# Attention of the later blocks in nine stops of two chunks each, inside a y, instead of seventeen stops of one

## The chip, the cores and the metric

One core of a Trainium2 chip runs the whole program in one launch. The metric is the device time of one execution in microseconds (us), read as the median of several runs. One execution was also taken by the hardware profiler; all rows below are of that one.

## The reference, cut to what matters

A decaying linear attention feeds two dense layers with different activations. 1536 tokens, model width 512, inner width 2048.

```python
# attention: B=2, H=8, S=768, D=64, blocks of 64
intra = (q_b @ k_b.T * Dmask) @ v_b                 # Dmask[i,j] = lam**(i-j) for i >= j
inter = (q_b * lam**(i+1)) @ kv_state
out_b = intra + inter
kv_state = lam**64 * kv_state + (k_b * lam**(63-i)).T @ v_b
# layer 0
h = x @ w_in;  g = where(h > 0, h, exp(min(h, 0)) - 1);  x = g @ w_out
# layer 1
h = x @ w_in2; P = a0 + a1*h + a2*h**2 + a3*h**3; Q = 1 + |b0|*|h| + |b1|*h**2
y = (P / (Q + 1e-6)) @ w_out2
```

## The kernel before

**Tiling of the layers.** The tokens are cut into three blocks of 512 (t = 0, 1, 2), the inner width into 16 groups of 128 (f = 0 to 15). A step is one (layer, t, f). In it TensorE (PE) makes h, 128 inner features by 512 tokens, from the block's x (`mlp_h`, 12 matmuls, line 435), and then the y of the step two before (`LAG = 2`; `mlp_y`, 12 matmuls into four banks, line 517). Twelve, because every fp32 operand is split into a high and a low part and three of the four products are made. Between the two, ScalarE (ACT) and VectorE (DVE) turn h into g: lines 448 and 449 (relu and exp, ACT), 450 (b, DVE, the last reader of h's PSUM bank), 452 (high part, ACT) and 453 (low part, DVE). h alternates between two PSUM banks, y has four, and two more (`pa0`, `pa1`) serve the attention.

**Weights of layer 0.** They arrive as raw 64-bit words, a pair of halves per f (`load_pair`, 1 MB, line 122; it lands in one of two alternating slots). DVE makes fp32 of them in three passes (lines 78, 81, 84), ACT rounds the high part (line 127), DVE subtracts for the low part (line 128). All of this is done during t = 0, a step or two ahead of its use, together with parking half of layer 1's weights in DRAM during t = 1 (`park_w2`).

**Attention.** Block 0's attention is the start-up. That of blocks 1 and 2, 16 chunks of 64 tokens (8 to 23), runs during the steps of t = 0 and t = 1, in *stops* (`att_visit`): for a new chunk n the products k·q (line 340), for the chunk d of the stop before the products with v (line 345), k·v for the state (line 351) and state·q (line 356), each 8 matmuls of 64 x 64 on a 64 x 64 quarter of the array. Then DVE masks n's products (line 376), POOL multiplies n's q by its powers (line 371), ACT takes d's output out of PSUM (line 384) and DVE adds the state (line 388). Stops stand at the steps in

```python
visits = [(3, 5, 7, 9, 10, 12, 13, 14, 15), (2, 4, 6, 8, 10, 12, 14, 15)]
```

between a step's h and its y: 17 of them, the first with n alone, the last with d alone.

**Order.** The instructions of t = 0 and 1 stand in the order of the code (`manual_schedule`); each engine works its own queue in that order. SyncE (SP) issues all the transfers, also in order: one that waits for its buffer holds up all behind it. Attention's `kv` has two buffers, `qk` two (a `qk` holds two chunks).

Of the kernel before, what the change touches and what calls it, by code (L numbers as in the profile page):

```python
# [16 lines left out]
P = 128  # L17
# [12 lines left out]
def fused_kernel(ctx, tc, lam, qkv, w1, w2, ab, out):  # L30
# [16 lines left out]
    ph = ctx.enter_context(tc.tile_pool(name="ph", bufs=2, space=PSUM))  # L47
# [252 lines left out]
    aa_tiles = []  # L300

    def sm_load_qk(k):

        c, row = k // 2, 4 * P
        qk = qq.tile([P, NP, 2, C], F32, tag="qk", name=f"qk{c}")
        src = qkv[c, 0, 0]
        for rho, r in enumerate(ROWS):
            nc.sync.dma_start(
                out=qk[r].rearrange("p (g a) x i -> p g (a x i)", a=2),
                in_=bass.AP(src.tensor, src.offset + (1 - rho) * D * row,  # L310
                            [[row, D], [2 * P * row, NP // 2], [1, row]]))

        for b in range(2):
            chunk[k + b] = {"q": qk[:, :, 0, b * CS:(b + 1) * CS],
                            "k": qk[:, :, 1, (1 - b) * CS:(2 - b) * CS]}

    def sm_load_kv(k):
        c, b, row = k // 2, k % 2, 4 * P
        chunk[k]["kv"] = kv = qq.tile([P, NP, 2, D], F32, tag="kv", name=f"kv{k}")
# [7 lines left out]
    def sm_products(n, d):  # L327

        if not aa_tiles:
            aa_tiles.extend(pa.tile([P, T], F32, tag=f"pa{i}", name=f"aa{i}")  # L330
                            .rearrange("p (x m i) -> p x m i", x=2, m=NP) for i in range(2))
            for r in ROWS:
                nc.tensor.matmul(aa_tiles[1][r, 1], lhsT=pick[r], rhs=mask64[r, :, 1:CS + 1],  # L333
                                 start=True, stop=True, skip_group_check=True)
            nc.scalar.activation(out=qpow[:, :, 0:CS], in_=aa_tiles[1][:, 1], func=AF.Copy)
        pn, pd = chunk.get(n), chunk.get(d)
        for m in range(NP):
            if pn:
                for r in ROWS:
                    nc.tensor.matmul(aa_tiles[0][r, 0, m], lhsT=pn["k"][r, m],  # L340
                                     rhs=pn["q"][r, m], start=True, stop=True,
                                     skip_group_check=True)
            if pd:
                for i, r in enumerate(ROWS):
                    nc.tensor.matmul(aa_tiles[1][ROWS[1 - i], 0, m], lhsT=pd["kv"][r, m, 1],  # L345
                                     rhs=pd["s"][r, m], start=m == 0, stop=d % KB == 0,
                                     skip_group_check=True)
        for m in range(NP):
            if pd and d % KB < KB - 1:
                for r in ROWS:  # L350
                    nc.tensor.matmul(aa_tiles[0][r, 1, m], lhsT=pd["kv"][r, m, 0],  # L351
                                     rhs=pd["kv"][r, m, 1], start=True, stop=True,
                                     skip_group_check=True)
            if pd and d % KB:
                for i, r in enumerate(ROWS):
                    nc.tensor.matmul(aa_tiles[1][ROWS[1 - i], 0, m], lhsT=state[r, m, 0],  # L356
                                     rhs=pd["q"][r, m], start=False, stop=True,
                                     skip_group_check=True)

    def sm_decay_k(n):  # L360

        kv = chunk[n]["kv"]
        if n % KB < KB - 1:
# [4 lines left out]
    def sm_decay_q(n):  # L368
        q = chunk[n]["q"]
        if n % KB:  # L370
            nc.gpsimd.tensor_tensor(out=q, in0=q, in1=qpow[:, :, 0:CS], op=ALU.mult)

    def sm_mask(n):
        b = chunk[n]
        b["s"] = s = ap_.tile([P, NP, CS], F32, tag="s", name=f"s{n}")
        nc.vector.tensor_tensor(out=s, in0=aa_tiles[0][:, 0], in1=mask64[:, :, 0:CS], op=ALU.mult)

    def sm_out(d):

        t, js = d * CS // T, slice(d * CS % T, d * CS % T + CS)  # L380
        if t not in xraw:
            xraw[t] = xr.tile([P, NP, T], F32, tag="xr", name=f"xr{t}")
        first, last = d % KB == 0, d % KB == KB - 1
        nc.scalar.activation(out=xraw[t][:, :, js], in_=aa_tiles[1][:, 0], func=AF.Copy)
        if first:
            nc.scalar.activation(out=state[:, :, 0], in_=aa_tiles[0][:, 1], func=AF.Copy)
        elif not last:
            nc.vector.tensor_tensor(out=state[:, :, 0], in0=aa_tiles[0][:, 1],
                                    in1=state[:, :, 1], op=ALU.add)

    def sm_decay_state(d):

        if d % KB not in (0, KB - 1):
            for m in range(NP):
                nc.scalar.activation(out=state[:, m, 1], in_=state[:, m, 0], func=AF.Copy,
                                     scale=qpow[:, m, CS - 1:CS])

# [102 lines left out]
    def mlp_y(layer, t, f):  # L500
# [27 lines left out]
    with ExitStack() as actx:  # L528
# [4 lines left out]
        qq = actx.enter_context(tc.tile_pool(name="qq", bufs=2))  # L533

# [20 lines left out]
        dmask = ac.tile([P, H, C + 1], F32, name="dmask")  # L555
        qpow = ac.tile([P, NP, C], F32, name="qpow")
        state = ac.tile([P, NP, 2, D], F32, name="state")

        mask64 = dmask.rearrange("p (m h) i -> p m h i", h=2)[:, :, 1, CS:]
# [8 lines left out]
        def make_qpow():  # L568
# [5 lines left out]
            def double(n):  # L574
# [4 lines left out]
        yy, hh = ((py, "y"),) * 2, ((ph, "h"),) * 2  # L579
        pp = (yy, hh, yy, yy, hh, yy, yy, ((ph, "h"), (pa, "pa0")))  # L580
# [4 lines left out]
        loads = [[(sm_load_qk, first), (sm_load_kv, first)], [(sm_load_kv, first + 1)],  # L585
                 [(sm_load_qk, first + 2)]]
        loads += [[(sm_load_kv, k + 1)] + [(sm_load_qk, k + 2)] * (k % 2 == 0 and k + 2 < end)
                  for k in range(first + 1, end - 1)]
        with tc.manual_schedule():
# [17 lines left out]
            for load, k in loads.pop(0):  # L607
                load(k)
# [43 lines left out]
            for h in range(5, H):  # L652
# [14 lines left out]
            low(2)  # L667
            s_part(4)
# [24 lines left out]
            att_hand(*atts[6])  # L693
            low(7)
# [3 lines left out]
            nc.gpsimd.tensor_copy(  # L698
                out=mask64[ROWS[1]],
                in_=dmask.rearrange("p (m h) i -> p m h i", h=2)[ROWS[1], :, 0, 0:CS + 1])  # L700
# [3 lines left out]
        h_pool = lambda: (ph, "h")  # L704
# [8 lines left out]
        def att_visit(due, more):  # L713

            n = todo.pop(0) if more and todo else None
            d = due.pop() if due else None
            sm_products(n, d)
            if n is not None:
                sm_mask(n)
                sm_decay_q(n)  # L720
                due.append(n)
            if d is not None:
                sm_out(d)
                del chunk[d]

        with tc.manual_schedule():
            due = []
            next_d = []
# [6 lines left out]
            visits = [(3, 5, 7, 9, 10, 12, 13, 14, 15), (2, 4, 6, 8, 10, 12, 14, 15)]  # L735
            assert sum(park_at.values()) == len(parks)
            for layer, t, f in steps(0, 0) + steps(0, 1):
                if f == 0 and t:
# [3 lines left out]
                    for n in due:  # L742
                        sm_decay_k(n)
                new = mlp_h(layer, t, f, later=True)
                queue.append((layer, t, f))
                if t or f != 1:
                    run(old, 2)
                    for d in next_d:
                        sm_decay_state(d)
                    next_d = []  # L750
# [27 lines left out]
                if f in visits[t]:  # L778
                    att_visit(due, t == 0 or f < NF - 1)
                    next_d = list(due)  # L780
                    for n in due:
                        if f < NF - 1:
                            sm_decay_k(n)
                for w in now if t or f else ():
                    run(w, len(w) - 1)
                if t == 0 and f + 2 < FULL:
                    load_pair(f + 2)
                elif t == 0 and f in (FULL, NF - 2, NF - 1):
                    load_raw(2 if f == FULL else 1)
                elif t == 0 and f in (FULL - 2, FULL - 1, FULL + 1):  # L790
                    load_pair(*{FULL - 2: (FULL + 1, NF - 3), FULL - 1: (FULL + 2, NF - 4),
                                FULL + 1: (FULL + 3, NF - 3)}[f])
                if loads and (f in visits[t][1 - t:] or t == 0 and f in (1, 2)):
                    for load, k in loads.pop(0):
                        load(k)
                if t == 0 and f == 3:
                    load_raw(2)
                lows = [op for w in now for op in w]
                if len(queue) > LAG:
                    mlp_y(*queue.pop(0))  # L800
# [10 lines left out]
    def h_pool():  # L811
        nh[0] += 1
        return ((ph, "h"), (ph, "h"), (pa, "pa0"), (pa, "pa1"))[nh[0] % 4]
# [89 lines left out]
```

## Time and profile before

| | us |
|---|---|
| median of 3 runs | 573.3 |
| lowest and highest | 572.07, 573.34 |
| the profiled execution, its own time | 572.56 |
| its span, first to last instruction | 570.8 |

PE is busy 99% of the span at a granted clock of 0.999 of full speed; DVE 81%, ACT 63%, POOL 5%. In the page's 40 slices DVE reads 9 or more from the second to the ninth (14 to 128 us, most of t = 0), and 5 to 7 in t = 1. The profile's own page says that a busy PE is not PE at its peak, so the rows below look at starts, and at the distance from one start to the next.

### The profile page before, as it was taken

The numbers are of one execution on the slowest core, as the hardware profiler recorded it, in microseconds if no ns is written. First come the engines' busy times: TensorE is split into PE (matmuls) and PEld (weight loads), VectorE is DVE, ScalarE is ACT, GpSimd is POOL, SyncE is SP. The second block draws the span as 40 slices with busy tenths as digits, with TensorE's granted clock in tenths as the row PEclk, the third lists the DMA queues.
The fourth block names the chain that finished last, engine by engine and source line by source line (L and its number), as shares of the span: only waits on it lengthen the run. The fifth ranks groups of instructions, "written<-read, shape, count | busy, mean of one in ns | idle before, by whom it ended". The sixth has DMA issues, their size and how long they took to land.

```text
span 570.8 us, 9255 instructions
## 1 busy us (share of the span) xinstructions
PE 564.6 (99%) x3550; PEld 464.9 (81%) x3550; DVE 464.7 (81%) x722; ACT 358.5 (63%) x690; POOL 29.8 (5%) x51
## 2 busy tenths in 40 slices
PE   8999999999999999999999999999999999999997
PEld 7877888888888888888888888888888888888885
DVE  6999999965676635877979999888898888898882
ACT  3746646875554545555568976667877666776672
POOL 7401001100100000000000000000000000000000
PEclk9999999999999999999999999999999999999999
DMA  8977677464687513434432500000400000200001
GB/s 291 318 225 243 237 227 214 107 206 128 204 240 229 165 49 136 167 135 177 150 108 78 182 3 1 1 2 0 145 3 2 0 1 0 75 0 1 1 1 74
DMA packets 41215, 64.58 MB, mean 113 GB/s; under 512 B 20178, under 2 KB 20178, under 8 KB 41170
## 3 DMA queue, kind: packets, MB, share of 16 engines
q1 hardware_dynamic: 41168, 63.98, 35.8%
q8 instruction: 28, 0.46, 0.3%
q14 instruction: 17, 0.14, 0.1%
q10 hardware_dynamic: 2, 0.00, 0.0%
HBM read 53.48 MB, written 10.49 MB: 112 GB/s over the span
## 4 chain that ended last, share of the span: by engine, by line
PE 98%; DMA 1%; SPq 0%; ACT 0%; issue 0%
PE h L435 46%; PE y L517 43%; PE y L426 3%; PE aa L340 1%; DMA att<-qkv_in 1%; PE aa L351 1%; PE pa L243 1%; PE pa L209 1%; PE pa L249 0%; PE aa L356 0%; PE aa L345 0%; SPq L192 0%; PE sums L256 0%; PE pa L291 0%; ACT o L487 0%; PE aa L333 0%
## 5 line engine op out<-in xcount | busy, mean ns | idle before, releaser
L435 PE MATMUL h<-xhi,w 128*128 128x512 f32 x768 | 204.8, 389 | 0.0
L517 PE MATMUL y<-ghi,w 128*128 128x512 f32 x712 | 191.8, 392 | 0.0
L435 PEld LDWEIGHTS h<-xhi,w 128*128 128x128 f32 x768 | 143.8, 188 | 30.3 <-DVE w L128 0.4
L517 PEld LDWEIGHTS y<-ghi,w 128*128 128x128 f32 x712 | 132.3, 188 | 27.8
L435 PE MATMUL h<-xlo,w 128*128 128x512 f32 x384 | 102.6, 389 | 0.0
L517 PE MATMUL y<-glo,w 128*128 128x512 f32 x356 | 95.3, 389 | 0.0
L435 PEld LDWEIGHTS h<-xlo,w 128*128 128x128 f32 x384 | 72.1, 188 | 15.0
L517 PEld LDWEIGHTS y<-glo,w 128*128 128x128 f32 x356 | 66.8, 188 | 14.2
L461 ACT ACTIVATE a<-h,babs 128x512 f32<-128x512 f32 x48 | 33.0, 688 | 63.8 <-PE h L435 63.8
L448 ACT ACTIVATE a<-h 128x512 f32<-128x512 f32 x48 | 28.3, 589 | 43.1 <-PE h L435 42.9
L465 DVE SCALAR_TENSOR_TENSOR b<-b,babs,a 128x512 f32<-128x512 f32 x48 | 36.0, 751 | 20.9 <-ACT b L462 20.7
L450 DVE SCALAR_TENSOR_TENSOR b<-a,h 128x512 f32<-128x512 f32 x48 | 32.7, 681 | 15.3 <-ACT a L449 12.1
L452 ACT ACTIVATE ghi<-b 128x512 fp32r<-128x512 f32 x48 | 30.0, 626 | 22.4 <-DVE b L450 22.4
L453 DVE TENSOR_TENSOR glo<-b,ghi 128x512 fp32r<-128x512 f32 x48 | 34.0, 709 | 7.0 <-ACT ghi L452 4.8
L463 ACT ACTIVATE p<-h,cab 128x512 f32<-128x512 f32 x48 | 37.7, 785 | 0.0
L467 ACT ACTIVATE a<-b,one 128x512 f32<-128x512 f32 x48 | 35.0, 729 | 3.1 <-DVE b L465 2.6
L469 DVE SCALAR_TENSOR_TENSOR p<-p,cab,h 128x512 f32<-128x512 f32 x48 | 35.8, 746 | 1.2
L473 DVE SCALAR_TENSOR_TENSOR b<-b,one,a 128x512 f32<-128x512 f32 x48 | 35.8, 746 | 0.1
L475 DVE SCALAR_TENSOR_TENSOR p<-p,cab,a 128x512 f32<-128x512 f32 x48 | 35.8, 746 | 0.0
L58 DVE TENSOR_TENSOR glo<-p,ghi 128x512 fp32r<-128x512 f32 x48 | 33.0, 688 | 3.0 <-PE y L426 1.5
L468 DVE TENSOR_TENSOR p<-p,h 128x512 f32<-128x512 f32 x48 | 32.8, 682 | 2.9 <-ACT p L463 2.9
L477 DVE SCALAR_TENSOR_TENSOR p<-b,p 128x512 f32<-128x512 f32 x48 | 33.1, 690 | 1.2
(88 smaller groups left out, 611.2 us busy)
## 6 DMA issues: line engine op xcount, KB each, us to landing
raw<-w_in SPq DMA_DIRECT2D x64, 512.0 KB, 4.5
att<-qkv_in SPq DMA_DIRECT2D x16, 256.0 KB, 6.0
qk<-qkv_in SPq DMA_DIRECT2D x16, 256.0 KB, 4.3
kv<-qkv_in SPq DMA_DIRECT2D x64, 64.0 KB, 4.0
w2d<-wbuf SPq DMA_DIRECT2D x16, 256.0 KB, 4.5
wbuf<-w2d SPq DMA_DIRECT2D x16, 256.0 KB, 2.8
x2d<-o SPq DMA_DIRECT2D x12, 256.0 KB, 2.3
x2r<-x2d SPq DMA_DIRECT2D x12, 256.0 KB, 3.1
```

Of the source, the lines that this page charges most:

```text
L58: lo_eng.tensor_tensor(out=lo, in0=src, in1=hi.bitcast(F32), op=ALU.subtract)
L435: nc.tensor.matmul(h, lhsT=w[:, a, 0, k * P:(k + 1) * P], rhs=xs[layer, t, k][b], start=i == k == 0, stop=i == 2 and k == NP - 1)
L453: lambda: nc.vector.tensor_tensor(out=glo, in0=b, in1=ghi.bitcast(F32), op=ALU.subtract)]
L461: nc.scalar.activation(out=a, in_=h, func=AF.Abs, scale=babs[:, 0:1])
L463: nc.scalar.activation(out=p, in_=h, func=AF.Identity, scale=cab[:, 3:4], bias=cab[:, 2:3])
L465: nc.vector.scalar_tensor_tensor(out=b, in0=b, scalar=babs[:, 1:2], in1=a, op0=ALU.mult, op1=ALU.add)
L467: nc.scalar.activation(out=a, in_=b, func=AF.Ln, bias=one[:, 0:1])
L469: nc.vector.scalar_tensor_tensor(out=p, in0=p, scalar=cab[:, 1:2], in1=h, op0=ALU.add, op1=ALU.mult)
L473: nc.vector.scalar_tensor_tensor(out=b, in0=b, scalar=one[:, 0:1], in1=a, op0=ALU.add, op1=ALU.mult)
L475: nc.vector.scalar_tensor_tensor(out=p, in0=p, scalar=cab[:, 0:1], in1=a, op0=ALU.add, op1=ALU.mult)
L477: nc.vector.scalar_tensor_tensor(out=p, in0=b, scalar=2.0, in1=p, op0=ALU.subtract, op1=ALU.mult, reverse0=True)
L517: nc.tensor.matmul(ys[layer, t][m], lhsT=w[:, a, 1, m * P:(m + 1) * P], rhs=g[b], start=f == i == 0, stop=False)
```

## The change

`att_visit` takes two chunks n, n+1 and the two of the stop before. Stops stand at nine steps, `at = [2, 5, 8, 11, 14, 18, 22, 26, 30]` counted over t = 0 and 1, and no more between h and y but inside `mlp_y`, after the seventh of its 12 matmuls. The outputs of the older pair go to the spare h bank (`ax`, the bank that the next step's h will take), so both banks of `pa` serve the new pair's k·q (`pa0`) and the k·v (`pa1`). Masks and q's decay are one instruction per pair, the output copy too; the state is added in two instructions, the second a step later (`sm_state`), and k·v of a chunk is made at the stop of the next pair. A table of powers (`pow64`) that the first stop made is made in the start-up (`sm_banks`). `kv` has three buffers.

At a stop's step the transfers of the next attention pair stand ahead of that step's raw weights (`load_w1`).

```diff
-    ph = ctx.enter_context(tc.tile_pool(name="ph", bufs=2, space=PSUM))
+    ph = ctx.enter_context(tc.tile_pool(name="ph", bufs=1, space=PSUM))
...
+    def sm_products(n, d, spare):
+
+        if d is not None:
+            aa_x[0] = spare.rearrange("p (m x i) -> p m x i", x=2, m=NP)
+        for j in range(2):
+            pn = chunk.get(n + j) if n is not None else None
+            pd = chunk.get(d + j) if d is not None else None
+            for m in range(NP):
+                if pn:
+                    for r in ROWS:
+                        nc.tensor.matmul(aa_tiles[1][r, j, m], lhsT=pn["k"][r, m],
+                                         rhs=pn["q"][r, m], start=True, stop=True,
+                                         skip_group_check=True)
+                if pd:
+                    for i, r in enumerate(ROWS):
+                        nc.tensor.matmul(aa_x[0][ROWS[1 - i], m, j], lhsT=pd["kv"][r, m, 1],
+                                         rhs=pd["s"][r, m], start=j == m == 0,
+                                         stop=(d + j) % KB == 0, skip_group_check=True)
+        for j in range(2):
+            c = n + j - 1 if n is not None else None
+            kv = chunk[c]["kv"] if c in chunk and c % KB < KB - 1 else None
...
     def sm_decay_q(n):
-        q = chunk[n]["q"]
-        if n % KB:
-            nc.gpsimd.tensor_tensor(out=q, in0=q, in1=qpow[:, :, 0:CS], op=ALU.mult)
+        q = chunk[n]["qk"][:, :, 0].rearrange("p m (b i) -> p m b i", b=2)
+        nc.gpsimd.tensor_tensor(
+            out=q, in0=q, in1=pow64.rearrange("p m (b i) -> p m b i", b=1)
+            .to_broadcast([P, NP, 2, CS]), op=ALU.mult)
...
+        nc.scalar.activation(out=xraw[t][:, :, js].rearrange("p m (b i) -> p m b i", b=2),
+                             in_=aa_x[0], func=AF.Copy)
...
-    def mlp_y(layer, t, f):
+    def mlp_y(layer, t, f, between=None):
...
+                if between and (i, m) == (1, 2):
+                    between()
...
+        vv = actx.enter_context(tc.tile_pool(name="vv", bufs=3))
...
+        at = [2, 5, 8, 11, 14, NF + 2, NF + 6, NF + 10, NF + 14]
+        pairs = list(range(first, end, 2))
+        loads = {}
+        for i, k in enumerate(pairs[1:]):
+            for j, load in enumerate(((sm_load_kv, k - 1), (sm_load_qk, k), (sm_load_kv, k))):
+                loads.setdefault(at[i] if i or j else 1, []).append(load)
...
+        def att_visit(s, f):
+
+            v = at.index(s)
+            spare = ph.tile([P, T], F32, tag=f"h{(f + 1) % 2}", name=f"ax{s}") if v else None
...
                 for w in now if t or f else ():
-                    run(w, len(w) - 1)
...
+                    run(w, len(w) - (2 if s in at else 1))
+                if s not in at:
+                    load_w1(t, f)
+                if len(queue) > LAG:
+                    mlp_y(*queue.pop(0), between=(lambda: att_visit(s, f)) if s in at else None)
...
+                for load, k in loads.get(s, ()):
+                    load(k)
+                if s in at:
+                    load_w1(t, f)
```

PE's queue around the first stop, before (a row is line, operation, out<-in, size; `aa` is a bank of `pa`):

```order
L435 MATMUL h_0_3_586<-xhi_0_0_261,w_1_508 128x512 x2
L435 MATMUL h_0_3_586<-xhi_0_1_285,w_1_508 128x512 x2
L333 MATMUL aa_613<-dmask,tabs 64x256 x2
L340 MATMUL aa_612<-qk_200 64x64 x8
L517 MATMUL y_0_0_570<-ghi_0_1_504,w_1_508 128x512
L517 MATMUL y_0_1_571<-ghi_0_1_504,w_1_508 128x512
```

And PE's queue around the first stop now, in step 2 (line 346 is k·q, 361 is k·v, 535 is y, 453 is h):

```order
L535 MATMUL y_0_2_579<-ghi_0_0_490,w_0_222 128x512
L535 MATMUL y_0_3_580<-ghi_0_0_490,w_0_222 128x512
L535 MATMUL y_0_0_577<-glo_0_0_491,w_0_222 128x512
L535 MATMUL y_0_1_578<-glo_0_0_491,w_0_222 128x512
L535 MATMUL y_0_2_579<-glo_0_0_491,w_0_222 128x512
L346 MATMUL aa_533<-qk_204 64x64 x16
L361 MATMUL aa_462<-kv_207 64x64 x8
L535 MATMUL y_0_3_580<-glo_0_0_491,w_0_222 128x512
L535 MATMUL y_0_0_577<-ghi_0_0_490,w_0_222 128x512
L535 MATMUL y_0_1_578<-ghi_0_0_490,w_0_222 128x512
```

The 8 small matmuls between h and y became 24 behind the seventh matmul of a y, and the two of line 333 stand in the start-up.

SP's queue from the first `kv` issued in the layers' steps to the raw weights of f = 8, before:

```order
L323 DMA kv_530<-qkv_in 64x4x64 x4
L122 DMA raw_4_564<-w_in 128x1024 x2
L308 DMA qk_567<-qkv_in 64x2x512 x2
L122 DMA raw_5_635<-w_in 128x1024 x2
L114 DMA raw_12_0_638<-w_in 128x1024
L114 DMA raw_10_1_640<-w_in 128x1024
L122 DMA raw_6_687<-w_in 128x1024 x2
L122 DMA raw_7_773<-w_in 128x1024 x2
L323 DMA kv_776<-qkv_in 64x4x64 x4
L122 DMA raw_8_826<-w_in 128x1024 x2
```

The same stretch of SP's queue now:

```order
L323 DMA kv_544<-qkv_in 64x4x64 x4
L308 DMA qk_621<-qkv_in 64x2x512 x2
L323 DMA kv_624<-qkv_in 64x4x64 x4
L122 DMA raw_4_629<-w_in 128x1024 x2
L122 DMA raw_5_666<-w_in 128x1024 x2
L122 DMA raw_6_722<-w_in 128x1024 x2
L323 DMA kv_849<-qkv_in 64x4x64 x4
L308 DMA qk_854<-qkv_in 64x2x512 x2
L323 DMA kv_857<-qkv_in 64x4x64 x4
L122 DMA raw_7_862<-w_in 128x1024 x2
L122 DMA raw_8_899<-w_in 128x1024 x2
```

raw_4 and raw_7 (the number is f) now stand behind six and ten issues of attention's inputs.

## Rows read from the trace of the kernel before

**Rows 1.** The page, part 4: the chain that ended last.
```profile
PE 98%; DMA 1%; SPq 0%; ACT 0%; issue 0%
```

**Rows 2.** Waits, PE's weight loads (engine, line, releaser: us in total, times, longest).
```profile
PEld aa L340 <- issue: 4.9, 14, 0.4
PEld h L435 <- DVE w L128: 0.4, 1, 0.4
```

**Rows 3.** Timeline, PE, the stop of step 7 (start us, duration us, engine, line).
```profile
59.12 1.07 PE L435 MATMUL h<-xhi,w 128*128 128x512 f32 x4
...
60.23 0.23 PE L340 MATMUL aa<-qk 64*64 64x64 f32 x2
...
61.05 0.23 PE L351 MATMUL aa<-kv 64*64 64x64 f32 x2
...
61.22 1.19 PE L517 MATMUL y<-ghi,w 128*128 128x512 f32 x4
62.25 1.08 PE L517 MATMUL y<-glo,w 128*128 128x512 f32 x4
```

**Rows 4.** The chain in order of time, two y of t = 0 (start us, us).
```profile
42.29 2.72 PE y L517 x12
...
61.28 2.95 PE y L517 x12
```

**Rows 5.** Instructions on tile aa, k·q (count of records; duration ns least, median, most).
```profile
L340 PE MATMUL aa<-qk x256: 215/218/267, 36.0 to 202.9; 64*64 64x64 f32 x128
```

**Rows 6.** Timeline, PE, the first stop.
```profile
35.51 0.65 PE L333 MATMUL aa<-dmask,tabs 64*64 64x256 f32 x4
35.99 0.63 PE L340 MATMUL aa<-qk 64*64 64x64 f32 x16
```

**Rows 7.** Timeline, PE and ACT, the last stop.
```profile
209.15 0.68 PE L345 MATMUL aa<-s,kv 64*64 64x64 f32 x16
209.26 0.60 ACT L448 ACTIVATE a<-h 128x512 f32<-128x512 f32 x1 [3.66 <-PE h L435]
...
210.42 0.37 ACT L384 ACTIVATE xr<-aa 128x256 f32<-128x256 f32 x1
```

**Rows 8.** Timeline, DVE, steps 4 to 7 (the bracket: idle before, and its releaser).
```profile
44.88 0.70 DVE L78 TENSOR_SCALAR w<-raw 128x1024 int32<-128x1024 int32 x1 [1.26 <-DMA raw<-w_in]
...
49.62 0.68 DVE L450 SCALAR_TENSOR_TENSOR b<-a,h 128x512 f32<-128x512 f32 x1
...
52.58 0.42 DVE L376 TENSOR_TENSOR s<-aa,dmask 128x256 f32<-128x256 f32 x1
52.92 0.42 DVE L388 TENSOR_TENSOR state<-aa,state 128x256 f32<-128x256 f32 x1
...
56.24 0.69 DVE L78 TENSOR_SCALAR w<-raw 128x1024 int32<-128x1024 int32 x1
...
61.59 0.68 DVE L78 TENSOR_SCALAR w<-raw 128x1024 int32<-128x1024 int32 x1
```

**Rows 9.** Timeline, SP's queue: issues of raw weights, qk and kv.
```profile
32.29 2.50 SPq L323 DMA_DIRECT2D kv<-qkv_in  x4
36.80 1.34 SPq L122 DMA_DIRECT2D raw<-w_in  x2
38.19 1.27 SPq L308 DMA_DIRECT2D qk<-qkv_in  x2
...
49.73 6.83 SPq L122 DMA_DIRECT2D raw<-w_in  x4
56.66 2.51 SPq L323 DMA_DIRECT2D kv<-qkv_in  x4
```

**Rows 10.** Transfers of line 122: from issue to landing.
```profile
DMA to landing us min/median/max: 3.1/4.8/10.0
```

**Rows 11.** Timeline, POOL and DVE beside each other in t = 1.
```profile
191.02 0.73 POOL L371 TENSOR_TENSOR qk<-qk,qpow 128x256 f32<-128x256 f32 x1 [11.28 <-PE aa L340]
...
191.05 1.25 DVE L453 TENSOR_TENSOR glo<-b,ghi 128x512 fp32r<-128x512 f32 x1
```

More of the change, by code (lines that the diff above doesn't have):

```diff
@@ L325, in sm_load_kv @@
                     [[row, CS], [P, 4], [1, D]]))
[L327 to L358, printed above, removed]
@@ L360, in sm_decay_k @@
     def sm_decay_k(n):
-        kv = chunk[n]["kv"]
-        if n % KB < KB - 1:
+        if n in chunk and n % KB < KB - 1:
+            kv = chunk[n]["kv"]
             for m in range(NP):
@@ L381, in sm_out @@
         if t not in xraw:
             xraw[t] = xr.tile([P, NP, T], F32, tag="xr", name=f"xr{t}")
[L383 to L389, printed above, removed]
@@ L391, in sm_decay_state, with sm_state @@
-    def sm_decay_state(d):
-        if d % KB not in (0, KB - 1):
+        nc.scalar.activation(out=xraw[t][:, :, js].rearrange("p m (b i) -> p m b i", b=2),
+                             in_=aa_x[0], func=AF.Copy)
+    def sm_state(n):
+        if n - 1 in chunk and n % KB:
+            j = n % 2
+            if n % KB == 1:
+                nc.scalar.activation(out=state[:, :, j], in_=aa_tiles[0][:, j], func=AF.Copy)
+            else:
+                nc.vector.tensor_tensor(out=state[:, :, j], in0=aa_tiles[0][:, j],
+                                        in1=state[:, :, 2], op=ALU.add)
@@ L584, in fused_kernel @@
         first, end = todo[0], todo[-1] + 1
[L585 to L588, printed above, removed]
+        at = [2, 5, 8, 11, 14, NF + 2, NF + 6, NF + 10, NF + 14]
[4 more added lines that the diff above has]
+                loads.setdefault(at[i] if i or j else 1, []).append(load)
+        loads.setdefault(at[-2], []).append((sm_load_kv, end - 1))
+        work, late, states = {}, {}, {}
+        for v, s in enumerate(at[:-1]):
+            k = first + 2 * v
+            if v:
+                late.setdefault(s - 1, []).extend((sm_decay_k, n) for n in (k - 1, k))
+            work.setdefault(s + 1, []).append((sm_decay_state, k))
+            states[s + 1] = k + 1
+            work.setdefault(s + 2 + (s + 2 == NF), []).append((sm_decay_state, k + 1))
         with tc.manual_schedule():
@@ L606, in fused_kernel @@
             load_pair(1)
-            for load, k in loads.pop(0):
-                load(k)
+            for load in (sm_load_qk, sm_load_kv):
+                load(first)
             def s_part(i):
@@ L693, in fused_kernel @@
             att_hand(*atts[6])
+            sm_banks()
             low(7)
@@ L711, in fused_kernel @@
         queue = []
[L713 to L717, printed above, removed]
+        def att_visit(s, f):
+            v = at.index(s)
+            spare = ph.tile([P, T], F32, tag=f"h{(f + 1) % 2}", name=f"ax{s}") if v else None
+            n = pairs[v] if v < len(pairs) else None
+            d = pairs[v - 1] if v else None
+            sm_products(n, d, spare)
+            if d is not None:
+                sm_out(d)
             if n is not None:
@@ L720, in att_visit @@
                 sm_decay_q(n)
-                due.append(n)
             if d is not None:
-                sm_out(d)
-                del chunk[d]
+                if n is not None:
+                    sm_state(n)
+                for j in range(2):
+                    del chunk[d + j]
         with tc.manual_schedule():
-            due = []
-            next_d = []
             lows = w
```

117 lines of the change are left out of this document (71 added, 46 removed).

## The prediction

> **What bounds the kernel now.** I read the chain that ended last first: PE holds 98% of it [rows 1], so only what shortens PE's queue, or makes PE wait, moves the time. Then the waits of PE: outside the start-up its weight loads wait for another engine once, for 0.4 us; the larger item is 4.9 us of "issue" in front of the first k·q matmul of 14 stops, 0.35 us each [rows 2]. So something is paid each time PE turns from the large matmuls to the small ones, though nothing is late. Third, the timeline of one stop, to price it. 12 large matmuls take 2.72 us [rows 4], 0.227 each. The last four of h start at 59.12, so without a stop y would begin at 60.03. Its fifth matmul starts at 62.25, where 60.03 + 4 x 0.227 = 60.94 was due: a full stop costs 1.31 us. Of that, the small matmuls go in pairs, one pair every 0.0586 us (14 spacings from 60.23 to 61.05), 16 pairs, 0.94 us; 0.37 us is left that does not depend on how many there are, before the first and around the return to y [rows 3]. Call a pair's place a slot. A matmul without a partner takes a slot too: the last stop's 8 matmuls with v (16 records) stand alone and are busy 0.68 us, less one duration of 0.22 that is 0.46 for 7.5 slots, 0.06 each [rows 5, 7].
>
> **The sum.** Before: 16 records per stop, 256 records, so 16 stops with k·q [rows 5], and one more with d alone; 17 in all. Slots: 16 x 16 + 8 = 264. With the table of powers in the first stop, 0.48 us from its start to that of k·q [rows 6]: 17 x 0.37 + 264 x 0.0586 + 0.48 = 6.29 + 15.47 + 0.48 = 22.24 us.
> After: nine stops. The first has 16 k·q and 8 k·v, none with a partner of the other kind: 24 slots. The other seven with new chunks have 16 + 16 paired and 16 more: 32. The last has 16 and 16 alone: 32. That is 280. 9 x 0.37 + 280 x 0.0586 = 3.33 + 16.41 = 19.74, and the table 0.48 in the start-up, where PE works on into the first h: 20.22 us.
> Difference: -2.02 us, which is 8 x 0.37 less 16 x 0.0586. Two places are not in the trace. The table in the start-up: nothing if PE would have waited there anyhow, at most another 0.37 if it makes a turn of its own; I take its 0.48. The turn inside a y instead of between h and y: the same change of matmuls on both sides, so 0.37; bounds 0.25 and 0.5, what one turn shows when the 0.12 lost on the return's four matmuls (1.03 for 0.91) is left out or paid twice, which is 1.1 us either way over nine stops.
>
> **What the small engines gain or lose, and what hides it.** Output copy: 16 ACT copies of 256 columns become 8 of 512. The masks on DVE: 16 of 0.34 (start to next start) become 8 of at most 0.68; the 13 state adds of 0.34 stay [rows 8]; POOL's 15 of 0.73 become 8 of about 1.46. A step with a weight pair costs DVE 5.35 us (from line 78 to the next, 56.24 to 61.59) against PE's 5.44. In three steps with one stop DVE has 16.05 + 0.68 + 0.68 = 17.4, PE 16.3 + 2.25 = 18.6, so DVE still gains 1.2 us on PE per stop. I cost all this at nothing. The cover is thin at three new meetings of queues.
>
> *The spare bank before the stop.* At stop s the products with v write the bank that h of step s-1 had, so they wait for b of step s-1 on DVE (line 450). Before, that b had until the next h, a stop and a y later. Behind PE's waiting matmul stands everything. Stop 5: in the old trace y ends and h5 begins at 45.01 [rows 4], and h5 ends at 47.73; by then the new kernel has paid 0.48 + 1.78 for the table and stop 2 instead of 0.48 + 0.84 for the first stop, so h5 ends at 48.67 and the bank is wanted 7 x 0.227 + 0.1 later, 50.4. b of step 4 ended at 49.62 + 0.68 = 50.30. DVE has 0.68 more in front of it (a pair's mask for a chunk's, and a state add), which goes into the 1.26 us in which it waited for the raw weights of f = 4, until 44.88 [rows 8]. So no stall, if those weights land as before. They are now issued behind qk and kv: 32.29 + 2.50 + 1.27 + 2.51 = 38.6 instead of 36.80 [rows 9], but qk, which followed and shared the engines with them, is then already away. Bounds of the landing: 0.7 us earlier (median of 4.8 behind the second issue at 39.4 [rows 10]) to 1.8 later; of the stall: 0 to 1.7. I take 0, near the median.
>
> *The raw weights behind the attention.* At stop 5 the kv and qk transfers need buffers that the stop's own products free, from about 51.0; they take 2.5 + 1.27 + 2.5 us of SP, so the pair of f = 7 goes out at 57.3 to 58.0, where it ended at 56.56 before, and lands 4.8 after the second issue at 57.65, at 62.4 [rows 9, 10]. DVE wants it at 61.59 plus the 0.68 that stop 5 adds, 62.3. b of step 7 then ends one step of 5.35 on, at 67.8. Stop 8 wants the bank at: h8 ends in the old trace at 61.28 + 2.95 + 2.72 = 66.95, shifted by 0.48 + 1.78 + 2.25 - 3.94 = +0.57, and 1.7 us on: 69.2. Slack 1.4 us. The pairs of stops 8 and 11 stand likewise. This slack is used up when a pair lands later than 6.2 us from issue; the measured longest is 10.0.
>
> *The spare bank after the stop.* The next h takes the bank as soon as the five last matmuls of y are through, 1.13 us plus about 0.1 after the products. ACT starts such a copy 0.1 us behind the products' end, and 512 columns from PSUM take 0.60 [rows 7]: 0.7 us. It is ready 0.5 us early, unless ACT is behind, and ACT is behind only when b was.
>
> POOL stands between. In the trace a DVE subtraction that started just behind POOL's 0.73 us product took 1.25 us [rows 11], where 512 columns take 0.68 [rows 8]: 0.57 lost to the overlap. With the doubled product the loss at one meeting lies between that 0.57 and 1.3 (1.46 less the same remainder); there are fewer meetings. I take the smaller, inside DVE's 1.2 us per stop.
> The Trainium skill, "SBUF — State Buffer", section "SBUF: two separate sides", says that the port pair of VectorE and GpSimd is an exclusive lock held for a whole instruction. The row agrees (DVE went on only after POOL's end), and by that rule the longer instruction costs DVE the 1.3, 0.7 more per meeting.
> At stop 5 the larger loss would leave 0.68 + 0.7 against 1.26 of cover, a stall of about 0.1.
>
> **Forecast.** -2.0 us on PE's queue, nothing else on the path: 572.56 - 2.0 = 570.5 in the profiled execution, which lies 0.7 under the median of 573.3; against that median 571.3. 0.3%, 1.7 us, is about what can be told from no change, so the forecast lies just beyond it. Its own range is 570.2 to 572.4, by the bounds of the turn.
>
> **Rivals.**
> 1. *DVE late at the spare bank*: the weights of f = 4 land by their later issue, or the lock takes more, and PE stalls about 1 us at stop 5, with remainders later. For it: no slack in the sum at stop 5. Against it: DVE's 1.2 us per stop. 573.3 - 2.0 + 1.0 = 572.3, within 0.3%.
> 2. *SP's queue makes PE wait; slower.* If the pairs behind the attention land midway between median and longest, 7.4 us from issue, each of stops 8, 11 and 14 meets a b that is 1.2 us late (7.4 less 6.2), 3.6 us together: 573.3 - 2.0 + 3.6 = 574.9. It decides from 6.2 us on; gain and loss cancel at 6.9. For it: f = 4 landed at 44.88, 7.4 us behind the second issue (36.80 + 0.67), when qk shared the engines. Against: now the attention goes first and is mostly moved before the pair starts.
> 3. *The change doesn't save the turns*: 0.37 belongs to 16 slots and not to a stop. Then 280 slots cost 0.94 more and nothing is saved: 574.2. Against it: the second half of a stop begins without a gap, one pair behind the other through 61.05 [rows 3], and the first stop with 8 slots paid a turn like the others.
>
> **Chances.** Forecast 0.50, rival 1 0.30, rival 2 0.14, rival 3 0.06. Faster by over 0.3%: 0.48, nearly all of the forecast. Within 0.3%: 0.36, rival 1 and what of the forecast and of rival 2 falls short. Slower by over 0.3%: 0.16, from rival 2, and rival 3 when it is at its worst. The range of 570.2 to 574.3 leaves out the upper half of rival 2 and little below.
>
> **What would show it.** Right: nine groups of small matmuls, about 2.25 us each from the seventh to the eighth matmul of a y beyond 0.23; "issue" in front of k·q falls from 14 x 0.35 to about 8; y and h groups of 2.72 everywhere else. Rival 1: PE's first matmul with v, or the h behind a stop, waits for DVE's b or ACT's output copy, at step 5 first. Rival 2: DVE's line 78 waits for raw weights at steps 7, 11 and 13 by over 1 us, and PE stands in the next stop. Rival 3: stops of 2.6 us and more with no releaser. The forecast is wrong if h0 itself begins over 0.8 us later, or if PE waits for over 0.5 us in all during t = 0 and 1.

## The result and the profile after

The changed kernel takes 575.5 us (median of 4 runs, 575.18 to 576.33), the kernel before 573.1 beside it (572.07 to 573.34): 1.0057 of its time, interval 1.0045 to 1.007. It is 2.4 us slower where 2.0 faster was forecast. The profiled execution has a span of 573.4 us, before 570.8, so 2.6 are to be found in it.

The chain that ended last, page part 4; before, PE held 98% of it [rows 1]:

```profile
PE 84%; DVE 8%; DMA 2%; SPq 2%; issue 1%; ACT 1%; DVEq 0%
```

A seventh of the chain has gone over to DVE and to what DVE waits for. Where, the waits of PE's weight loads tell (in total, times, longest); against them stand the two rows of before [rows 2]:

```profile
PEld aa L346 <- issue: 2.5, 7, 0.4
PEld ax L351 <- DVE b L468: 1.9, 3, 0.8
...
PEld y L535 <- ACT o L505: 1.1, 4, 0.3
PEld h L453 <- ACT xhi L57: 1.0, 3, 0.3
PEld h L453 <- DVE w L128: 0.5, 1, 0.5
```

The first row is the gain: 7 turns in front of k·q instead of 14 (the other two of the nine stops, and three of the seventeen before, are booked under other names, 0.35 to 0.4 us each). The other four are new or larger, 4.5 us; two small ones (0.4 for b in front of an h at 218 us, 0.2 for xlo) make it 5.1. Less the 0.4 that waited before and the 2.0 of the forecast, 2.7 is left, the 2.6 of the spans.

The gain itself is there. The timeline of PE, the stop of step 22, where nothing is late:

```profile
156.95 1.07 PE L535 MATMUL y<-ghi,w 128*128 128x512 f32 x4
157.85 0.84 PE L535 MATMUL y<-glo,w 128*128 128x512 f32 x3
158.63 0.27 PE L346 MATMUL aa<-qk 64*64 64x64 f32 x2
...
160.65 0.50 PE L535 MATMUL y<-glo,w 128*128 128x512 f32 x1
160.99 1.09 PE L535 MATMUL y<-ghi,w 128*128 128x512 f32 x4
```

The ninth matmul of this y was due at 156.95 + 8 x 0.227 = 158.77 and begins at 160.99: a stop of 2.22 us, where 0.37 + 32 x 0.0586 = 2.25 was worked out. Nine such groups stand in the trace.

Now the stop of step 8, on PE and then on DVE:

```profile
69.61 0.33 PE L346 MATMUL aa<-qk 64*64 64x64 f32 x4
70.49 0.27 PE L351 MATMUL ax<-s,kv 64*64 64x64 f32 x2 [0.55 <-DVE b L468]
```

```profile
62.97 0.68 DVE L468 SCALAR_TENSOR_TENSOR b<-a,h 128x512 f32<-128x512 f32 x1
65.02 0.69 DVE L78 TENSOR_SCALAR w<-raw 128x1024 int32<-128x1024 int32 x1 [1.36 <-DMA raw<-w_in]
...
69.76 0.68 DVE L468 SCALAR_TENSOR_TENSOR b<-a,h 128x512 f32<-128x512 f32 x1
```

PE has begun the stop and its first product with v waits for the spare bank, that is for b of step 7. DVE ends that b at 70.44, after it had waited 1.36 us for the raw weights of f = 7; before, it waited so at f = 4, 1.26 us [rows 8], where PE didn't wait for the b behind it. b was forecast for 67.8, the stop's need for 69.2. The issues behind it, SP's queue; before, the pairs of f = 6 and 7 went out from 49.73 to 56.56, ahead of kv [rows 9]:

```profile
51.44 2.50 SPq L323 DMA_DIRECT2D kv<-qkv_in  x4
54.05 1.93 SPq L308 DMA_DIRECT2D qk<-qkv_in  x2
56.08 2.51 SPq L323 DMA_DIRECT2D kv<-qkv_in  x4
58.69 1.02 SPq L122 DMA_DIRECT2D raw<-w_in  x2
```

The pair goes out 1.4 us later than the earliest time worked out (57.3) and lands at 65.0, 2.6 later than forecast.

The second thing that holds DVE, POOL beside it (before, 0.73 and 1.25 [rows 11]):

```profile
71.70 1.63 POOL L380 TENSOR_TENSOR qk<-qk,pow 128x512 f32<-128x512 f32 x1 [18.19 <-PE ax L351]
...
72.11 1.78 DVE L471 TENSOR_TENSOR glo<-b,ghi 128x512 fp32r<-128x512 f32 x1
```

A subtraction of 0.69 us takes 1.78. So it goes at stops 2, 5, 8 and 11 (1.77 to 1.79), and at stop 14 another instruction of 0.42 takes 1.39: 1.1 us lost at four stops of t = 0 and 1.0 at the fifth. Before, only three of the eight products of t = 0 cost DVE anything, 0.3 to 0.5 us each (alone these instructions take 1.22 and 1.23):

```profile
40.05 1.70 DVE L81 SCALAR_TENSOR_TENSOR w<-raw,w 128x1024 int32<-128x1024 int32 x1
...
73.57 1.76 DVE L128 TENSOR_TENSOR w<-w,w 128x1024 fp32r<-128x1024 f32 x1
...
99.10 1.57 DVE L128 TENSOR_TENSOR w<-wbuf,w 128x1024 fp32r<-128x1024 f32 x1 [0.52 <-ACT w L127]
```

The third stands on ACT, in front of the first y of t = 1, then on PE's weight loads:

```profile
129.26 2.01 ACT L375 ACTIVATE kv<-kv,mask 128x64 f32<-128x64 f32 x8
131.18 2.02 ACT L505 ACTIVATE o<-y 128x512 f32<-128x512 f32 x4
```

```profile
131.81 0.19 PEld L535 LDWEIGHTS y<-ghi,w 128*128 128x128 f32 x1 [0.20 <-ACT o L505]
132.29 0.19 PEld L535 LDWEIGHTS y<-ghi,w 128*128 128x128 f32 x1 [0.30 <-ACT o L505]
```

The eight decays of kv for the stop of step 18 are issued in step 17, ahead of the copies that empty y's four banks. PE has ended that y at 129.2; the next y wants the banks at 131.8 and waits four times, 1.1 us.

### The profile page after: what moved, and what is told of

It reads as the page before. It is cut to its first block, busy times and chain, and to the rows that moved or that the text cites. A ratio compares the mean times of both kernels' runs of the same rounds, so it can differ in the third digit from the quotient of the medians.

```text
span 573.4 us, 9238 instructions
## 1 busy us (share of the span) xinstructions
PE 566.7 (99%) x3550; PEld 466.8 (81%) x3550; DVE 468.2 (82%) x714; ACT 358.9 (63%) x682; POOL 29.0 (5%) x45
## 4 chain that ended last, share of the span: by engine, by line
PE 84%; DVE 8%; DMA 2%; SPq 2%; issue 1%; ACT 1%; DVEq 0%
PE h L453 39%; PE y L535 37%; PE y L444 3%; DMA raw<-w_in 2%; DVE w L128 2%; DVE glo L471 1%; DVE w L81 1%; SPq L323 1%; PE pa L209 1%; PE pa L243 1%; DVE w L84 1%; DMA qk<-qkv_in 1%; DVE wbuf L84 1%; ACT w L127 1%; DVE wbuf L81 1%
## 5 line engine op out<-in xcount | busy, mean ns | idle before, releaser
L535 PE MATMUL y<-glo,w 128*128 128x512 f32 x356 | 97.6, 392 | 0.0
L471 DVE TENSOR_TENSOR glo<-b,ghi 128x512 fp32r<-128x512 f32 x48 | 37.2, 778 | 9.2 <-ACT ghi L470 8.3
```

The source lines that it names most:

```text
L471: lambda: nc.vector.tensor_tensor(out=glo, in0=b, in1=ghi.bitcast(F32), op=ALU.subtract)]
```

## The experiments

Theories: T1, POOL's doubled product holds DVE up by 1.1 us per stop, so b is late at the spare bank. T2, the raw weights behind the attention land late. T3, the stop inside the first y of t = 1 leaves that y to wait for ACT. The runs are from several chips, on each of them beside runs of the kernel before, whose median there was 572.0 to 572.2; ratios are to it, and 1.0057 would be 575.3. Where two rows differ by a few tenths of a microsecond, the ratios with their intervals decide and not the medians.

| edit to the changed kernel | us | ratio, interval |
|---|---|---|
| no q product | 573.0 | 1.0016, 1.0004 to 1.0027 |
| raw weights first | 574.6 | 1.0046, 1.0031 to 1.0061 |
| both | 571.4 | 0.9994, 0.9985 to 1.0002 |
| stop 18 between h and y | 578.1 | 1.0097, 1.0083 to 1.0112 |
| decays in step 16 | 574.9 | 1.0051, 1.0034 to 1.0068 |
| decays in 16, stop 18 between | 576.4 | 1.0071, 1.0059 to 1.0083 |
| q product on DVE | 575.4 | 1.0058, 1.0039 to 1.0077 |
| raw first, decays in 16 | 573.5 | 1.0024, 1.0015 to 1.0034 |
| the same, q product in two halves | 573.2 | 1.0021, 1.0012 to 1.0029 |
| the same, no q product | 571.0 | 0.998, 0.997 to 0.9989 |
| the same, q product on DVE | **570.9** | 0.9982, 0.9973 to 0.999 |
| the same, on DVE in t = 0 alone | 571.1 | 0.9983, 0.9974 to 0.9992 |
| best, table of powers in stop 2 | 571.9 | 0.9995, 0.9986 to 1.0004 |

### The q product left out

```diff
                 sm_mask(n)
-                sm_decay_q(n)
```

> Leaves out POOL's multiplication of q by the powers of lambda (so the output lacks that factor); nothing else. T1 (POOL's doubled product, 1.63 to 1.82 us, holds up the DVE instruction beside it by some 1.1 us per stop, so b of the step before the next stop is late and PE's products with v wait for it): the five DVE instructions of 1.39 to 1.79 us beside it go back to 0.42 to 0.68, the waits of PE at stops 8 and 14 (0.84 and 0.91) fall below 0.3 and the one at the first step of the next block (0.87) shrinks; 575.5 - 2.0 to 2.8 = 572.7 to 573.5. T2 (the raw weights behind the attention land late): the 1.36 us at step 7 stays, PE still waits about 0.8 at stop 8; 575.5 - 0.5 = 575.0. T3 (the stop inside the first y of t = 1 makes y wait for ACT's copies): its 1.07 us stay, 575.5 if it were all.

573.0, in T1's range. PE's waits now:

```profile
PEld y L535 <- ACT o L505: 0.9, 3, 0.3
PEld ax L351 <- DVE b L468: 0.7, 1, 0.7
```

Of three waits for b one is left, at stop 8, where DVE still waited 2.2 us for raw weights; the wait in front of ACT's copies stays, so it has its own cause. T1 carries most of the loss, not all.

### The raw weights first

```diff
-                if s not in at:
-                    load_w1(t, f)
+                load_w1(t, f)
                 if len(queue) > LAG:
...
-                if s in at:
-                    load_w1(t, f)
```

> The raw weights of a stop's step are issued ahead of the attention's transfers again, all else as in the changed kernel. T2: DVE's wait of 1.36 us for the raw weights at step 7 goes, and with it PE's wait at stop 8 and what DVE carries on from it to stop 14 and the next block; 575.5 - 2.0 to 2.5 = 573.0 to 573.5. T1: only the 1.36 us of DVE goes, of which 0.84 stands in front of PE at stop 8; DVE is still 1.1 us behind per stop, so the waits at stop 14 and at the block's end stay or fall by half; 575.5 - 0.5 to 1.0 = 574.5 to 575.0. T3: no change beyond that.

574.6, what T1 expected of it; the intervals don't tell this gain of 0.6 us from none. Stop 8 no longer waits, but stops 11 and 14 do, since DVE still loses 1.1 us per stop:

```profile
PEld ax L351 <- DVE b L468: 1.8, 2, 1.1
...
PEld y L535 <- ACT o L505: 1.1, 4, 0.3
PEld h L453 <- ACT xhi L57: 1.0, 3, 0.3
```

### Both

> Leaves out POOL's multiplication of q (the output lacks that factor) and issues the raw weights ahead of the attention at a stop's step. Alone the first gave 2.3 us and the second 0.6. T1 and T2 as separate causes: without POOL's product only the late raw weights of step 7 made PE wait (0.54 at stop 8), so 573.0 - 0.5 = 572.5 on that chip, 1.0007 of the kernel before; what is left above 570.0 (the forecast there) is the 1.1 us in front of the y of step 18, and the start-up and end, 0.3 each. If they were one cause (the weights late only because POOL's lock shifts the order): 573.0, no change.

571.4, lower than either number expected: 3.6 us below 1.0057, where the two alone sum to 2.9 (2.3 and 0.6). With the product gone, the raw weights first give 1.3 us (1.0016 to 0.9994, intervals apart), so T2 is a cause of its own. That fits two causes of which each alone leaves the other to fill part of its room; the excess of 0.7 us itself is within the intervals. PE no longer waits for b at any stop; one wait of 0.6 us for b, in front of the h at 215 us, is left.

### Stop 18 between h and y

```diff
+                if s in (NF + 2,):
+                    att_visit(s, f)
                 if len(queue) > LAG:
...
+                          if s in at and s not in (NF + 2,) else None)
```

> Only the first stop of t = 1 (step 18) is put between h and y again, the other eight stay inside y. T3 (the y behind it needs four banks whose copies ACT ends late, and the stop, 2.25 us of PE's own work, no longer stands in front of it): PE's wait of 1.1 us for ACT's copies in front of that y goes; 575.5 - 1.0 = 574.5. Against T3 (the wait only moves to the bank that the stop's products take, which frees with b of the step before): 575.5. T1 and T2 expect no more than T3 here, as nothing before step 18 is touched.

578.1, slower than either number expected: T3 as I had put it falls. The y no longer waits for ACT, but the stop does, longer (PE, then DVE):

```profile
136.07 0.27 PE L351 MATMUL ax<-s,kv 64*64 64x64 f32 x2 [1.67 <-DVE b L468]
```

```profile
135.32 0.69 DVE L468 SCALAR_TENSOR_TENSOR b<-a,h 128x512 f32<-128x512 f32 x1 [5.92 <-DMA x2d<-o]
```

b of step 17 waits until o has gone to DRAM, and o is what ACT copies late. One cause behind both waits was the next theory, T3a: the eight decays in front of the copies. The edit accounts for 1.67 - 1.1 = 0.6 us; at stop 14, which it doesn't touch, PE waited 1.8 instead of 0.6 us, for raw weights that DVE got 1.5 us late. That all five runs were that slow isn't explained by the edit, and stays open.

### The decays one step earlier, alone and with that stop moved

```diff
-                late.setdefault(s - 1, []).extend((sm_decay_k, n) for n in (k - 1, k))
+                late.setdefault(s - 1 - (s == NF + 2), []).extend((sm_decay_k, n) for n in (k - 1, k))
```

> Only the eight ACT decays of the k half of kv for the stop of step 18 are issued one step earlier, in step 16 instead of 17. In the changed kernel they take 2.01 us of ACT (129.26 to 131.2) right in front of the four copies of o, which start at 131.18 though PE ended the block's last y at 129.2; PE's y of step 18 then waits 1.1 us for the banks. T3a (the decays in front are what makes the copies late): the copies start some 1.4 to 2.0 us earlier, the 1.1 us go, 575.5 - 1.0 = 574.5 (relative to the kernel before: 1.0057 falls to about 1.004). T3b (the copies would be late anyway, since the stop no longer stands in front of that y): at most 0.3 us come back.

> The decays of step 17 one step earlier and, besides, the first stop of t = 1 between h and y again. Alone, that second edit made PE wait 1.67 us at step 18 for b of step 17, which DVE began at 135.32 after a wait of 5.9 us that ended with the transfer of o to DRAM. T3a (one cause for both: the copies of o, and so their transfer, start 2 us late behind the decays): that wait falls below 0.3 us, and the time is that of the earlier decays alone, within 0.5 us: 574.5. T3b (b of step 17 is late for a reason of its own, DVE's own work): the wait of 1.2 us or more stays.

ACT with the decays earlier:

```profile
126.58 2.01 ACT L375 ACTIVATE kv<-kv,mask 128x64 f32<-128x64 f32 x8
...
131.11 2.04 ACT L505 ACTIVATE o<-y 128x512 f32<-128x512 f32 x4
```

This trace runs 1.5 us later than the one above in front of this place (PE's h of step 16), so the copies are 1.6 us earlier, and the row of y waiting for ACT is gone: the mechanism is T3a. In the time it shows by 0.3 us only, which is T3b's number. In the profiled execution DVE got the raw weights of f = 4 and 7 later (1.25 and 1.87 us of wait against 0.51 and 1.36); whether that holds for the other executions isn't known. By itself, then, inconclusive in time. The cleaner pair is raw weights first without and with it: 1.0046 and 1.0024, 1.2 us, with intervals that just overlap. With stop 18 between h and y the wait for b fell from 1.67 to 0.76 us, not below 0.3, and the time is 1.1 us above that of the earlier decays alone (1.0071 and 1.0051), where T3a allowed 0.5: the decays are about half of that wait, the rest stays open, and the place inside y is the better one.

### The q product on DVE

```diff
-        nc.gpsimd.tensor_tensor(
+        nc.vector.tensor_tensor(
             out=q, in0=q, in1=pow64.rearrange("p m (b i) -> p m b i", b=1)
```

> The multiplication of q by the powers runs on DVE in place of POOL; the numbers are the same. T1: DVE pays the product itself, 1024 columns, about 0.7 to 1.3 us by the rows of 512 columns (0.34 to 0.68), in place of the 1.1 us that the overlap costs it; a gain of 0 to 0.4 us per stop, 575.5 - 0 to 1.5 = 574.0 to 575.5. If the overlap costs DVE nothing on the path (T2 or T3 alone), DVE has 0.7 to 1.3 us more per stop and the waits at stops 8 and 14 grow by as much: 576.5 to 578.

575.4, no gain, at the end of T1's range. DVE pays 0.6 (the product has 512 columns, not 1024) for 1.1, but is then only earlier at the raw weights (DVE, then PE, step 13 and stop 14):

```profile
105.98 0.69 DVE L78 TENSOR_SCALAR wbuf<-raw 128x1024 int32<-128x1024 int32 x1 [2.19 <-DMA raw<-w_in]
```

```profile
110.32 0.27 PE L351 MATMUL ax<-s,kv 64*64 64x64 f32 x2 [1.76 <-DVE b L468]
```

### The three together, and the q product taken back

> Three edits: q multiplied on DVE (0.61 us from start to start, measured) instead of beside POOL (1.1 us lost), raw weights ahead of the attention, and the decays of step 17 one step earlier. T1 + T2 + T3a: DVE has 0.5 us less per stop than in the changed kernel and no wait for raw weights, so the waits at stops 8, 11 and 14 go but for 0.5 us in all, and the 1.1 us at step 18 go: 570.0 (forecast on that chip) + 0.3 + 0.3 + 0.5 = 571.1, 0.998 of the kernel before. If any of the three is not the cause, about 1 us more each: 572 to 574. With q on DVE alone the raw weights of steps 4 and 13 were late (0.4 and 2.2 us), which the new order should remove.

570.9: faster than both kernels, 0.18% below the one before, under what I had called the least that can be told, though the interval of this comparison ends at 0.999. Its chain has PE at 95%, and no stop waits for b:

```profile
PEld aa L346 <- issue: 2.8, 8, 0.4
...
PEld h L453 <- ACT xhi L57: 0.6, 2, 0.3
PEld y L535 <- DVE glo L471: 0.6, 1, 0.6
```

> The raw weights ahead of the attention and the decays of step 17 one step earlier, with the q product on POOL as in the changed kernel: of the three edits that together gave 570.85, the one on the q product is missing. T1 (POOL's doubled product costs DVE 1.1 us each time it runs beside it): PE waits for b at stops 11 and 14 (0.9 and 0.6 when only the weights were moved) and for the block's first h (0.9), so 570.9 + 2.4 = 573.3, or 1.002 of the kernel before. If the product was harmless and the other two edits did all of it: 570.9, 0.998.

573.5: the q product back on POOL costs 2.4 us by the ratios (1.0024 and 0.9982; 2.7 by the medians), the 2.4 expected of T1. PE waits for b at two stops again, 11 and 14:

```profile
PEld ax L351 <- DVE b L468: 1.9, 2, 1.2
```

What DVE meets at stop 8 there:

```profile
69.97 1.80 POOL L380 TENSOR_TENSOR qk<-qk,pow 128x512 f32<-128x512 f32 x1 [16.91 <-PE ax L351]
...
70.54 2.31 DVE L128 TENSOR_TENSOR w<-w,w 128x1024 fp32r<-128x1024 f32 x1
```

An instruction of 1.23 us takes 2.31, the same 1.1.

> As the kernel with raw weights first and decays earlier, q on POOL, but its product as two instructions of 256 columns (0.73 us each before) in place of one of 512. If one DVE instruction is held up for what is left of one POOL instruction and DVE goes on between the two, each stop costs 0.5 us where both are not met, 573.3 - 1.2 = 572.1; if the second half holds DVE up as the first does, the sum is the same 1.1 us and the time is that of the long product, 573.3 +- 0.4.

```diff
+        for b in range(2):
+            nc.gpsimd.tensor_tensor(out=q[:, :, b], in0=q[:, :, b], in1=pow64, op=ALU.mult)
```

573.2, the same as the long product. POOL and DVE at stop 8:

```profile
69.45 2.56 POOL L381 TENSOR_TENSOR qk<-qk,pow 128x256 f32<-128x256 f32 x2 [15.82 <-PE ax L351]
69.65 1.75 DVE L128 TENSOR_TENSOR w<-w,w 128x1024 fp32r<-128x1024 f32 x1
71.33 1.23 DVE L470 TENSOR_TENSOR glo<-b,ghi 128x512 fp32r<-128x512 f32 x1
```

The two engines take turns (alone, line 128 takes 1.23 us and line 470 0.69): DVE loses 0.52 to the first half and 0.54 to the second.

> Leaves out the q product altogether (the output lacks the factor), with raw weights first and decays earlier: the change with its three losses taken away. If the ledger is complete (T1, T2, T3a and nothing else but 0.3 us at the start-up and 0.3 at the end of t = 1): forecast 570.0 on that chip + 0.6 = 570.6, 0.9975 of the kernel before, and no wait of PE over 0.3 us from 22 to 218 us. If a loss is still missing in it, the time stays above 571.2.

571.0, level with the product on DVE (570.9). So with the other two losses gone DVE's 0.6 us per stop are free. The time lies between the 570.6 of a complete ledger and the 571.2 of a missing loss, and one wait is left, in front of the h at 215 us:

```profile
PEld h L453 <- DVE b L468: 0.5, 1, 0.5
```

The kernel before has no such wait. It comes with the change, and its cause is open.

```diff
-        nc.gpsimd.tensor_tensor(
+        (nc.vector if n < pairs[5] else nc.gpsimd).tensor_tensor(
```

> As the best kernel so far (q on DVE, raw weights first, decays earlier), but the q product of the four stops of t = 1 on POOL again, where DVE waits for weights by several us a step. In the best kernel one y of t = 1 waited 0.6 us for DVE's glo behind the q product. T1 says that the overlap matters only where DVE is late: the 0.6 go and nothing comes in their place, 570.85 - 0.5 = 570.3. If POOL's overlap still costs 1.1 per stop there: 571 to 573.

571.1, no difference from the best; T1's 570.3 is missed, and the time alone doesn't tell it from the 571 to 573 of the other answer. In the trace y's wait for glo falls from 0.58 to 0.17 us, and the one for b in front of the h at 214 us rises from 0.18 to 0.53. Of the three products of t = 1 only one held a DVE instruction up, by 1.0 us, and no wait of PE follows it before that h:

```profile
180.15 1.65 DVE L84 SCALAR_TENSOR_TENSOR wbuf<-raw,wbuf 128x512 int32<-128x512 int32 x1
```

Beside the product at 155.71 DVE's mask of 512 columns, one of whose inputs lies in PSUM, took its usual 0.69, and POOL its 1.28.

### Where the rest of the 2.0 is

> The best kernel (q on DVE, raw weights first, decays earlier: 570.85), with the four matmuls of the table of powers and their ACT copy in the first stop again, where the kernel before has them, instead of the start-up. If the table is what the start-up loses (0.58 us in front of the first h, and a turn of PE's own there): the first h begins by 0.6 us earlier and the first stop is 0.48 us longer, 570.75; up to 0.4 better if the turn is saved too, 570.4. If the start-up differs by chance alone: 570.9, no change.

571.9, slower than the best by 0.7 us in the ratios (0.9995 and 0.9982) and 1.1 in the medians, and above all three numbers expected. The first h does begin earlier, at 20.63, but the copy of the table on ACT stands behind other work and the first stop waits for it:

```profile
34.15 0.56 PE L364 MATMUL aa<-kv 64*64 64x64 f32 x12 [1.34 <-ACT pow L337]
```

So the start-up is the better place for the table as it is made here.

> The kernel before, unchanged, for a profile on the chip on which the experiments ran. If the missing 0.9 us is a matter of the chip: the span here is about 569.9 (570.8 less 0.9) and the first h begins at 21.0 as in the first profile. If it is in the changed kernel's start-up: the span is 570.8 again and the first h begins at 20.5 or earlier.

A span of 570.4 and the first h at 20.87, between the two answers; this chip is the one of the table in stop 2, not that of the other experiments. Compared with the changed kernel without its three losses, the first h and one h behind the last stop, kernel before:

```profile
20.87 0.96 PE L435 MATMUL h<-xhi,w 128*128 128x512 f32 x3
...
229.00 0.84 PE L435 MATMUL h<-xhi,w 128*128 128x512 f32 x3
```

and the other:

```profile
21.87 0.65 PE L332 MATMUL aa<-mask,tabs 64*64 64x256 f32 x4
22.45 0.72 PE L453 MATMUL h<-xhi,w 128*128 128x512 f32 x2
...
228.35 0.84 PE L453 MATMUL h<-xhi,w 128*128 128x512 f32 x3
```

208.13 us against 205.90: 2.23 us gained behind the first h, where the forecast has 2.0 + 0.48 = 2.5, with 0.5 us of waiting for b still in it. The table costs 22.45 - 21.87 = 0.58 in front of it, 0.48 forecast. That makes 1.65; the medians give 1.1, by the interval 0.6 to 1.7. The 2.23 is the high end: with the product on DVE the same distance is 206.65 (best kernel) and 206.41 (on DVE in t = 0 alone), 1.5 and 1.7 us gained. The first h itself began at 20.95 to 22.45 us in the profiles of the changed kernel and its variants that have the table in the start-up; in two of these traces PE waited 0.4 and 0.5 us there for a first load, the rest of the spread isn't explained. A remainder of half a microsecond is within that.

## Why the prediction was wrong

**What bounds the kernel now** and **the sum on PE's queue** were right: nine stops, 2.22 for 2.25 us, eight turns fewer. What failed is "nothing else on the path".

**The step that failed first**: "I take the smaller, inside DVE's 1.2 us per stop". The smaller was 0.57; the loss beside POOL's doubled product is 1.1 us, near the 1.3 of the upper end, at four stops of t = 0, and 1.0 at the fifth. "There are fewer meetings" failed with it: of the eight products of t = 0 before, three held DVE up, 1.35 us in all; of the five now all did, 5.3 us. (The slices of t = 0 in which DVE reads 9 or more end at 114 us, not at 128; all five meetings lie before.) With 1.1 of the 1.2 gone, DVE no longer gains on PE at a stop, and every later wait goes to PE undiminished. Taking the product away gave 2.3 us alone and 2.5 with the other two losses gone. At stop 8 POOL ends at 73.33 and DVE's 512 columns at 73.89, 0.56 later, and two halves cost what one whole does. The upper end was too high because the doubled product takes 1.28 us where it meets no such DVE instruction (t = 1), not 1.46; 1.28 less the prediction's remainder of 0.16 is 1.1, an estimate.

The Trainium skill, "SBUF — State Buffer", section "SBUF: two separate sides", has the port pair of VectorE and GpSimd as an exclusive lock for a whole instruction. The traces agree with it in kind: DVE's instruction ends 0.56 us behind POOL's, as above.

**The raw weights behind the attention**: slack 1.4 us at stop 8 by the text. The pair went out 1.4 us late (58.69 for 57.3), because qk took 1.93 for 1.27 on SP and kv began 0.4 later, and landed 2.6 late. Its landing at 65.0 is about 5.8 us behind its second issue at 59.2, less than the 6.2 that were to decide; what was late were its issue and DVE itself, which came to it at 63.66 (65.02 less 1.36) instead of 62.3, most of that the 1.1 lost beside POOL at stop 5. DVE then lost 1.36, and PE stood for it twice: 0.5 us in front of the h of step 8, for the low part of weights that DVE makes right behind (line 128), and 0.8 at the stop. This was rival 2, but not as I priced it: not each of three stops late by the landing, but one, on top of POOL.

**The spare bank before the stop**: for stop 5 b was worked out for 50.30 and wanted at 50.4. It was ready at 50.62, and PE's weight loads waited 0.4:

```profile
49.94 0.68 DVE L468 SCALAR_TENSOR_TENSOR b<-a,h 128x512 f32<-128x512 f32 x1
```

The sum was right to 0.3 us, and the conclusion "no stall" had no margin to rest on. Without the q product PE doesn't wait at this stop.

**What no step had**: three thin places were named, the one at step 18 wasn't. The eight decays that the change issues in step 17 stand in no list of the text, not even among what it costs at nothing; I didn't ask what is queued behind them on ACT. The answer, y's copies, cost 1.1 us; moving the decays gave 1.2 back with the raw weights first, and 0.3 alone.

**The rivals**: rival 1 had the mechanism, DVE late at the spare bank, with one stall of 1 us and remainders; it came three times (stops 5, 8 and 14), with the block's first h, which waits for ACT, as a fourth. Rival 2's time, 574.9, is nearest to the 575.5, but the weights put first gave back only 0.6 of it alone. Rival 3 is ruled out by the stop of 2.22 us; its price left out that the 16 more slots would bring their share of the 0.37 too, 1.3 us in all instead of 0.94. A third of the forecast's own range (570.2 to 572.4) lies within 0.3% of 573.3, so "faster by over 0.3%" could not get nearly all of the forecast's chance. The mistake in the chances was to treat rivals 1 and 2 as alternatives: they delay the same b, and add once the slack is used up.

## What to carry to other kernels

Price an overlap by what the delayed engine owes next: if the bounding engine now waits on the spot for a result that earlier had a stage of slack, take the upper end, however well the average balance looks. For each instruction that a change moves, list what stands behind it on its own queue and who waits for that, also on an engine that is busy only 63% of the time. When two delays meet at one wait, take both away before judging either: here the product left out gave 2.3 us alone, the raw weights first 0.6, and moving the product to DVE alone nothing; that move together with the two other edits turned 2.4 us slower into 1.0 us faster.

## What the runs showed of the hardware

- A product of 512 columns from SBUF takes POOL 1.63 to 1.82 us in t = 0 of the changed kernel, where DVE is busy beside it (1.28 to 1.44 in t = 1 with the product on DVE in t = 0 alone), and DVE 0.68; worked out were 1.46. Moved to DVE it costs 0.6; left on POOL it costs DVE 1.0 to 1.1 at each stop of t = 0.
- Cutting POOL's product in halves changes nothing: 0.52 + 0.54 us lost instead of 1.1, and 573.2 us for 573.5.
- It isn't only instructions with two operands that are held up: line 78, one operand, took 1.39 instead of 0.42. And not every one with two is: the mask, with one input in PSUM, took 0.69 beside POOL's 1.28 at 155.72.
- PE's turn from large to small matmuls is paid per group, not per matmul: 4.9 / 14 = 0.35 us in front of k·q with 16 slots a stop [rows 2], 2.5 / 7 = 0.36 with 24 or 32.
